# S4 convolution plus gated MLP on one core: a new written-out order of 1281 tasks, with the Exp table, the identity and one token block's statistics moved

## The chip, the cores and the metric

The kernel runs on one core of a Trainium2 chip. The metric is device time in microseconds (us) of one execution. Three runs of the kernel before took 268.34 us in the median (267.07 to 268.83).

## What is computed

A token matrix u (2048 tokens x 512 channels, bfloat16) is layer-normalised to xn. Two branches read xn, and the result is u + A(xn) + B(xn).

```
xn = (x - mean) / sqrt(var + 1e-5)
# A: a diagonal state-space model as a long convolution, per channel d
dt = exp(log_dt);  K[d, l] = Re sum_n C[d,n] * exp(dt[d] * (A_re + i A_im)[d,n] * l) * dt[d] * B[d,n]
yA = irfft(rfft(xn, 4096) * rfft(K, 4096))[:2048] + xn * Dskip
# B: a gated MLP with 1792 hidden units
yB = (sigmoid(xn @ w_gate) * (xn @ w_up)) @ w_down
```

## The kernel before, in words

**Layer norm.** The tokens lie in four groups (`xg`, 0 to 3) of four blocks of 128 tokens. A block's statistics come from VectorE's batch-norm instruction (`stat`, L443, for group 0 with an aggregation, L445) or, for blocks 1 and 3 of group 0, as an alternative from three ACT instructions that sum as they go (`stat_act`, L449 to L451). Group 0's reciprocal deviation is computed on VectorE (`rstd0`, L457 to L470). That of group 1, and that of groups 2 and 3 together, is computed on GpSimd (`rstd`, 33 small instructions each, L479 to L510). Then each block is normalised (`norm` on VectorE, L514, or `norm2` on ACT, L519). Groups 0 and 1 are transposed on PE (L524), groups 2 and 3 by DMA transposes from SP's queue (L547), into `xnT`.

**Parameters.** `params` computes dt with ACT's Exp (L596), scales the identity with it to `dg` (L597, on VectorE), and multiplies the raw parameters by it on PE (L608, banks `ptd` and `pb`); C is only transposed there (L613, `ptp`, evicted as `raw`). Exponentials (L621), a range reduction on VectorE (`turns`, `frac`, L632 to L637), an Abs (L646) and Sin (L640, L641) on ACT give the complex base powers, which are squared (L663 to L672) and multiplied to tables `M` and `B`. ACT loads three function tables: Exp (ahead of the warm-up in L594), Sin, Sigmoid (at L807).

**The two branches.** Eight chunks of 64 channels: `tables` builds the powers H and G by doubling on VectorE (L1244 to L1246, with squares on ACT and VectorE, L888 to L892), PE multiplies them to the kernel K (`pk`, L976), the spectrum steps follow (L762 `pz` for x, L946 to L1026 for K, L1078 `px`), products in the frequency domain (L1125 `pkf`, L1145, L1133 and L1136 `pv`), and the way back (L1192, L1206 to L1212, `ptv`, `py`). The gated MLP runs over four groups of 512 tokens and seven pairs of hidden tiles: `pg` and `pu` on PE (L781), a sigmoid of `pg` on ACT (L807), an eviction of `pu` on ACT, the product on VectorE (L814 or L819), then the down product `po` (L785), its evictions `gs` and `gl`, and an accumulating DMA from GpSimd's queue (L840). `pg` and `pu` share two buffers, so a pair cannot start before the evictions of the pair before it.

**The order.** Nothing is scheduled when the kernel is built. Each `add` makes a task, numbered in the order of the calls, with an engine, a planned cost in us and perhaps an alternative (another engine, cost and function). `TURN` is the written-out order in which the tasks are emitted, and so the order of the instructions on every engine's in-order queue and of the DMA issues on SP's, ACT's and GpSimd's. `OTHER` lists the tasks that take their alternative. A planner that is not part of the kernel made both from the planned costs; when the kernel is built, the costs themselves do nothing:

```python
def order(self):
    for t in (self.tasks[n] for n in OTHER):
        t.eng, t.cost, t.fn = t.alt[:3]
    return [self.tasks[n] for n in TURN]
```

Waits come from the data and the buffers. Tasks that are spoken of later: 0 and 1 load x's blocks 0-1 (SP) and 2-3 (ACT), 2 the identity, 3 the constant s1 (both GpSimd), 4 log_dt, 5 to 10 the raw parameters (6, 10 and 8 on ACT), 11, 12, 14, 15 and 18 to 21 the gate and up weights, 13, 16 and 17 x's groups 1, 2 and 3 (SP). 26 to 29 are group 0's statistics, 30 is rstd0, 43 and 60 are GpSimd's two rstd. 101 fills constants on GpSimd, 103 is the Exp warm-up, 104 dt, 105 dg, 106 to 110 PE's parameter products.

Of the kernel before, what the change touches and what calls it, by code (L numbers as in the profile page):

```python
# [13 lines left out]
ACT = mybir.ActivationFunctionType  # L14
# [237 lines left out]
class _Kernel:  # L252
# [180 lines left out]
    def layernorm(self):  # L433
        nc, add, c = self.nc, self.p.add, self.mult
# [92 lines left out]
        for lo, hi in ((0, 1), (1, 2), (2, 4)):  # L527
            st = [add("DVE", 0.69 if lo else 0.87, lambda i=i: stat(i), [self.ld[f"x{i // 4}{i // 2 * 2 if i < 4 else 0}"]],
                      R["LN2"] + i if lo else R["LN"], use=[self.xg[i // 4]], alt=("ACT", 1.5, lambda i=i: stat_act(i), R["LN"]) if i in (1, 3) else None)
                  for i in range(4 * lo, 4 * hi)]  # L530
            slow = lambda lo=lo, hi=hi: rstd(lo, hi, nc.gpsimd)
            r = add("POOL", 20.0, slow, st, R["LN2"] + 10 * lo) if lo == 1 else add(
                "DVE", 4.2 if lo else 3.4, (lambda lo=lo, hi=hi: rstd(lo, hi, nc.vector)) if lo else rstd0, st, R["LN2"] + 10 * lo if lo else R["LN"],
                alt=("POOL", 16.0, slow, R["LN2"] + 10 * lo) if lo else None)
# [697 lines left out]
def _level(nc, l, o, m, tB, rs, step):  # L1232
# [124 lines left out]
```

## Time and profile before

| what | value |
|---|---|
| time, median of 3 (range) | 268.34 us (267.07 to 268.83) |
| the profiled execution's own time | 268.08 us |
| its span in the trace | 266.3 us |
| PE busy, 2040 matmuls | 236.8 us (89%) |
| VectorE (DVE) busy, 450 instructions | 240.3 us (90%) |
| ACT busy, 369 instructions | 227.8 us (86%) |
| GpSimd (POOL) busy, 107 instructions | 65.7 us (25%) |
| moved by DMA | 44.38 MB, mean 167 GB/s |
| granted TensorE clock, mean | 0.99 |

How to read it: the span is the profiled time between the first and the last instruction; the execution's own time is 1.78 us longer. A row of a timeline has its start, its length, the engine, the line of the kernel, the operation with output and input tiles, and in square brackets the idle time of the engine before it with what ended that. PE, PEld (PE's weight loads), DVE, ACT, POOL and SP are the engines; a q behind a name is its sequencer, which issues DMAs. The chain that ended last is the way back from the last instruction: at each step to what released it, or else to the instruction before it on its engine. Since all engines are in-order, an instruction that waits holds up everything behind it on its engine.

### The profile page before, as it was taken

The page shows a single profiled execution, that of the slowest core. Times are in us where ns is not written, and L with a number is a line of the kernel's source. Part 1 is how long each engine was busy: PE and PEld are TensorE (multiplying, and loading weights), DVE is VectorE, ACT ScalarE, POOL GpSimd, SP SyncE. Part 2 cuts the span into 40 slices and gives each one's busy share as a digit, 9 for nine tenths or more (in the row PEclk, how much of TensorE's full clock was granted, in tenths as well). Part 3 has the DMA queues.
Part 4 walks back from the last instruction along what each step waited for, and adds up shares of the span by engine and source line. Part 5 has one row for each costly group of instructions (what it writes and reads, how often), then busy time and mean ns, then how long its engine had stood idle before and what let it go on. Part 6 is the DMA issues. An engine that isn't in the chain of part 4 may idle for free.

```text
span 266.3 us, 5528 instructions
## 1 busy us (share of the span) xinstructions
PE 236.8 (89%) x2040; PEld 137.4 (52%) x2040; DVE 240.3 (90%) x450; ACT 227.8 (86%) x369; POOL 65.7 (25%) x107
## 2 busy tenths in 40 slices
PE   0556899998799999999999999999998988988992
PEld 0432345443345545545544654665656575567771
DVE  1699999996999999999999999999999999986860
ACT  3989999979987864799897599999999989998851
POOL 4007977884300003100000210000001020207451
PEclk9999999999999999999999999999999999979998
DMA  7729977101692114589424579888798997979898
GB/s 223 265 81 295 337 232 223 39 2 15 166 258 76 54 40 56 101 183 190 131 87 152 115 166 209 233 216 224 193 272 185 290 218 200 245 152 174 172 95 99
DMA packets 75467, 44.38 MB, mean 167 GB/s; under 512 B 40064, under 2 KB 72064, under 8 KB 74928
## 3 DMA queue, kind: packets, MB, share of 16 engines
q1 hardware_dynamic: 66000, 39.66, 54.7%
q0 software_dynamic: 6752, 3.31, 11.8%
q10 hardware_dynamic: 2688, 1.05, 1.6%
q8 instruction: 16, 0.26, 0.4%
q14 instruction: 11, 0.09, 0.1%
HBM read 24.61 MB, written 15.73 MB: 151 GB/s over the span
## 4 chain that ended last, share of the span: by engine, by line
PE 44%; DVE 21%; ACT 20%; POOL 6%; issue 5%; DMA 1%; ACTq 0%; DVEq 0%; POOLq 0%
PE pg L781 11%; PE pu L781 10%; PE po L785 5%; DVE tB L1244 4%; PE pk L976 4%; DVE G L1245 3%; ACT M L361 2%; PE pv L1136 2%; DVE G L1246 2%; DVE H L1245 2%; ACT hT L807 2%; PE pz L762 2%; PE py L1209 2%; PE pv L1133 2%; PE pkf L1125 2%
## 5 line engine op out<-in xcount | busy, mean ns | idle before, releaser
L781 PEld LDWEIGHTS <-W 128*128 128x128 bf16 x448 | 43.2, 98 | 55.5 <-issue 8.2
L781 PE MATMUL pg<-xnT,W 128*128 128x512 bf16 x224 | 52.9, 379 | 4.0 <-ACT hT L807 3.3
L781 PE MATMUL pu<-xnT,W 128*128 128x512 bf16 x224 | 52.9, 379 | 1.7 <-DVE db L658 1.4
L840 POOL DMA_DIRECT2D out_dram<-gs x16 | 13.7, 874 | 156.9 <-ACT gs L361 94.7
L785 PE MATMUL po<-wd,hT 128*128 128x512 bf16 x224 | 51.2, 379 | 0.0
L785 PEld LDWEIGHTS <-hT 128*128 128x128 bf16 x224 | 21.4, 98 | 22.8 <-issue 0.2
L888 ACT ACTIVATE tB<-G 128x1024 bf16<-128x1024 bf16 (+2 forms) x25 | 30.4, 1214 | 3.1 <-DVE G L892 2.5
L807 ACT ACTIVATE hT<-pg 128x1024 bf16<-128x1024 f32 x28 | 29.3, 1045 | 1.8 <-DVE hT L814 0.8
L361 ACT ACTIVATE hT<-pu 128x1024 bf16<-128x1024 f32 x24 | 24.9, 1039 | 1.3 <-PE pu L781 1.2
L1246 DVE TENSOR_TENSOR G<-G,tB 128x512 bf16<-128x512 bf16 (+2 forms) x35 | 22.3, 641 | 0.3
L1245 DVE TENSOR_TENSOR G<-G,M 128x512 bf16<-128x512 bf16 (+2 forms) x50 | 20.5, 451 | 0.1
L976 PEld LDWEIGHTS <-G 128*128 128x128 bf16 x512 | 17.4, 98 | 4.4 <-DVE G L1246 1.0
L976 PE MATMUL pk<-H,G 128*128 128x64 bf16 x512 | 18.4, 193 | 1.1 <-ACT B L361 0.7
L361 ACT ACTIVATE zs<-pz 128x512 bf16<-128x512 f32 x30 | 17.3, 609 | 2.3 <-PE pz L762 2.3
L1145 DVE TENSOR_TENSOR M<-XX,M 128x1024 bf16<-128x1024 bf16 x28 | 18.9, 684 | 0.3 <-ACT M L361 0.3
L1244 DVE TENSOR_TENSOR tB<-G,M 128x512 bf16<-128x512 bf16 (+2 forms) x27 | 18.9, 705 | 0.2
L1246 DVE TENSOR_TENSOR H<-H,tB 128x512 bf16<-128x512 bf16 (+2 forms) x24 | 18.6, 775 | 0.2
L361 ACT ACTIVATE M<-pkf 128x512 bf16<-128x512 f32 x26 | 16.7, 659 | 0.9 <-PE pkf L1125 0.9
L361 ACT ACTIVATE ksb<-pk 128x512 bf16<-128x512 f32 x28 | 16.5, 627 | 0.9 <-PE pk L978 0.7
L814 DVE TENSOR_TENSOR hT<-hT 128x1024 bf16<-128x1024 bf16 x24 | 16.4, 684 | 0.6 <-ACT hT L361 0.5
L361 ACT ACTIVATE Z<-pzk 128x512 bf16<-128x512 f32 x23 | 13.7, 616 | 2.6 <-PE pzk L946 2.6
L1133 PE MATMUL pv<-M,w 128*128 128x256 bf16 (+1 forms) x128 | 14.6, 251 | 1.1 <-DVE M L1145 1.1
(206 smaller groups left out, 477.3 us busy)
## 6 DMA issues: line engine op xcount, KB each, us to landing
z_scr<-zs SPq DMA_DIRECT2D x32, 128.0 KB, 1.8
XX<-XX SPq DMA_DIRECT2D x28, 128.0 KB, 4.1
zk_scr<-Z SPq DMA_DIRECT2D x3, 1024.0 KB, 7.0
B<-zk_scr SPq DMA_DIRECT2D x12, 256.0 KB, 4.4
B<-z_scr SPq DMA_DIRECT2D x8, 256.0 KB, 3.4
wd<-in_B_w_down_dram SPq DMA_DIRECT2D x1, 1792.0 KB, 13.0
xg<-in_A_u_dram SPq DMA_DIRECT2D x3, 512.0 KB, 5.7
W<-in_B_w_up_dram SPq DMA_DIRECT2D x3, 512.0 KB, 7.0
```

What stands on the lines that cost most here:

```text
L361: return self.p.add("ACT", cost, lambda: nc.scalar.activation(out=dst(), in_=src(), func=ACT.Identity), alt=alt and ("DVE", alt[0], lambda ...
L781: nc.tensor.matmul(p[:, kk, :], w(kt, kk), xnT[:, kt, :], start=(kt == 0), stop=(kt == KT - 1))
L785: nc.tensor.matmul(po[:], hT[:, k, jj * 128:(jj + 1) * 128], wd[:, k, :], start=(k == 0), stop=False)
L807: e1 = add("ACT", 1.03, lambda hT=hT, k=k, pg=pg: nc.scalar.activation(out=hT[:, k:k + 2, :], in_=pg[:], func=ACT.Sigmoid), [m1] + held.ge ...
L814: prods.append(add("DVE", 0.69, lambda hT=hT, u=u, k=k: nc.vector.tensor_tensor(out=hT[:, k:k + 2, :], in0=hT[:, u:u + 2, :], in1=hT[:, k: ...
L888: a = add("ACT", 0.22 + 4 * h * k / 1200.0, lambda: nc.scalar.activation(out=sv(), in_=G[:, :, rs, src, :], func=ACT.Square, scale=float(2 ...
L976: nc.tensor.matmul(pk[:, r], G[:, comp, 8 * q + r].rearrange("p a h -> p (a h)"), H[:, comp, 8 * q + r].rearrange("p b h -> p (b h)"), sta ...
L1133: nc.tensor.matmul(pv[:, n, :], w, pp[:, i, n, :], start=(i == 0), stop=(i == 1))
L1145: d = add("DVE", 0.69, lambda pp=pp, XX=XX, k1=k1, bs=bs: nc.vector.tensor_tensor(out=pp[:], in0=XX[:, :, bs, dx], in1=k1[:].to_broadcast( ...
L1244: lambda: [tt(out=tv()[:, c], in0=l[:, c], in1=mul[1][:, c], op=ALU.mult) for c in cs],
L1245: lambda: [tt(out=inner(o[:, c]), in0=inner(l[:, c]), in1=both(c), op=ALU.mult) for c in ones],
L1246: lambda: [tt(out=o[:, c], in0=o[:, c], in1=tv()[:, flip(c)], op=ALU.add) for c in cs],
```

## The change

Three planned costs are set anew: ACT's statistics of a block from 1.5 to 1.75 us, GpSimd's rstd of group 1 from 20.0 to 19.2 and of groups 2 and 3 from 16.0 to 20.0, rstd0 from 3.4 to 3.35. These numbers do not reach the instructions. `TURN` and `OTHER` are replaced, and with them the order on all engines. In the opening:

- ACT: the Exp warm-up (103) and dt (104) stand ahead of ACT's fifth load issue (8) instead of behind it.
- GpSimd: the identity (2) and s1 (3) are issued first, the constants (101) are filled after them.
- Block 1's statistics (27) go from ACT to VectorE, and stand first there; block 3's (29) stay on ACT.
- PE: the last `pb` product (109) stands ahead of the first `pz` (184) instead of behind it.
- SP: x's group 2 (16) is loaded after three writes of `z_scr` and the weight loads 11, 12 and 15, instead of ahead of them.

Further on, all 1281 tasks are in a new order, and 77 tasks besides 27 change sides between their two forms, mostly evictions between ACT and VectorE. In the middle of the kernel, four of the copies `H<-B` and `G<-B` that start a table (L906) go from VectorE to ACT, and two the other way; several evictions of `pk`, `pz` of K and `px` go from ACT to VectorE. ACT's norms of groups 2 and 3 (L519, tasks 61, 71, 81, 92, 72, 91) stand behind the evictions of three of group 0's four `po` tiles; before, 71, 62, 82 and 92 stand behind the first of these alone, and 62 and 82 are VectorE's now, 81 ACT's. The same values are computed from the same inputs; VectorE has three aggregations (L445) in place of two, and ACT one set of statistics instructions (L449 to L451) in place of two.

```diff
-  ... alt=("ACT", 1.5, lambda i=i: stat_act(i), R["LN"]) if i in (1, 3) else None)
+  ... alt=("ACT", 1.75, lambda i=i: stat_act(i), R["LN"]) if i in (1, 3) else None)
...
-            r = add("POOL", 20.0, slow, st, R["LN2"] + 10 * lo) if lo == 1 else add(
-                "DVE", 4.2 if lo else 3.4, (lambda lo=lo, hi=hi: rstd(lo, hi, nc.vector)) if lo else rstd0, st, R["LN2"] + 10 * lo if lo else R["LN"],
-                alt=("POOL", 16.0, slow, R["LN2"] + 10 * lo) if lo else None)
+            r = add("POOL", 19.2, slow, st, R["LN2"] + 10 * lo) if lo == 1 else add(
+                "DVE", 4.2 if lo else 3.35, (lambda lo=lo, hi=hi: rstd(lo, hi, nc.vector)) if lo else rstd0, st, R["LN2"] + 10 * lo if lo else R["LN"],
+                alt=("POOL", 20.0, slow, R["LN2"] + 10 * lo) if lo else None)
...
 TURN = (
-    0, 4, 102, 101, 1, 5, 6, 7, 10, 2, 8, 9, 103, 22, 13, 3, 17, 16, 26, 104, 27, 105, 29, 28, 106, 112, 107, 30,
-    114, 111, 115, 113, 110, 121, 11, 108, 117, 116, 36, 31, 184, 23, 32, 109, 185, 118, 187, 33, 188, 175, 120, 172,
...
+    0, 4, 102, 2, 1, 5, 6, 3, 7, 10, 9, 103, 104, 27, 26, 22, 101, 105, 8, 29, 28, 106, 111, 107, 112, 113, 114, 115,
+    110, 13, 17, 30, 121, 11, 108, 109, 117, 116, 36, 31, 184, 32, 187, 185, 118, 175, 33, 176, 172, 119, 34, 177,
+    186, 188, 120, 12, 173, 189, 35, 122, 15, 41, 37, 16, 42, 14, 166, 39, 174, 123, 40, 18, 38, 43, 181, 20, 124,
...
 OTHER = (
-    27, 29, 38, 44, 60, 61, 62, 71, 72, 82, 91, 92, 143, 144, 145, 148, 149, 155, 158, 160, 161, 227, 239, 301, 316,
...
+    29, 38, 49, 60, 61, 71, 72, 81, 91, 92, 144, 146, 148, 155, 158, 160, 161, 224, 257, 306, 361, 371, 416, 497,
...
```

More of the change, by code (lines that the diff above doesn't have):

```diff
@@ L528, in layernorm @@
             st = [add("DVE", 0.69 if lo else 0.87, lambda i=i: stat(i), [self.ld[f"x{i // 4}{i // 2 * 2 if i < 4 else 0}"]],
-                      R["LN2"] + i if lo else R["LN"], use=[self.xg[i // 4]], alt=("ACT", 1.5, lambda i=i: stat_act(i), R["LN"]) if i in (1, 3) else None)
+                      R["LN2"] + i if lo else R["LN"], use=[self.xg[i // 4]], alt=("ACT", 1.75, lambda i=i: stat_act(i), R["LN"]) if i in (1, 3) else None)
                   for i in range(4 * lo, 4 * hi)]
             slow = lambda lo=lo, hi=hi: rstd(lo, hi, nc.gpsimd)
-            r = add("POOL", 20.0, slow, st, R["LN2"] + 10 * lo) if lo == 1 else add(
-                "DVE", 4.2 if lo else 3.4, (lambda lo=lo, hi=hi: rstd(lo, hi, nc.vector)) if lo else rstd0, st, R["LN2"] + 10 * lo if lo else R["LN"],
-                alt=("POOL", 16.0, slow, R["LN2"] + 10 * lo) if lo else None)
+            r = add("POOL", 19.2, slow, st, R["LN2"] + 10 * lo) if lo == 1 else add(
+                "DVE", 4.2 if lo else 3.35, (lambda lo=lo, hi=hi: rstd(lo, hi, nc.vector)) if lo else rstd0, st, R["LN2"] + 10 * lo if lo else R["LN"],
+                alt=("POOL", 20.0, slow, R["LN2"] + 10 * lo) if lo else None)
             self.rstd.append(r)
```

119 rows, old and new, of tables (OTHER, TURN) are left out of this document.

## The prediction

> **What bounds the kernel now.** I read the page, then the table of stages, then the chain of work, then the rows at the places the chain names. The page first: its span, and the busy tenths in 40 slices of 6.7 us.
>
> ```profile
> span 266.3 us, 5528 instructions
> PE   0556899998799999999999999999998988988992
> DVE  1699999996999999999999999999999999986860
> ACT  3989999979987864799897599999999989998851
> ```
>
> No engine is idle for long: PE, VectorE and ACT stand at 8 to 9 tenths nearly throughout. What is left lies at the start, around slice 9 (60 to 67 us), and in the tail. The stages show it in us (length, then busy time of PE, PE's weight loads, VectorE, ACT, GpSimd, each with its count of instructions):
>
> ```profile
> 0.00:20.00 20.00, 7.54 (x43) 5.91 (x44) 12.30 (x39) 13.96 (x27) 3.25 (x11) 1.00 0.60 190
> 20.00:41.00 21.00, 17.51 (x83) 7.69 (x81) 20.59 (x25) 20.80 (x26) 16.07 (x33) 1.00 0.95 290
> 62.00:90.00 28.00, 25.26 (x179) 12.63 (x178) 24.95 (x45) 24.59 (x36) 3.16 (x4) 1.00 0.52 129
> 90.00:130.00 40.00, 39.95 (x285) 20.26 (x283) 39.17 (x72) 31.73 (x51) 3.38 (x4) 1.00 0.54 115
> 160.00:200.00 40.00, 39.67 (x326) 24.21 (x324) 39.88 (x67) 39.19 (x64) 0.00 (x0) 1.00 0.90 224
> ```
>
> PE loses 12.5 us in the first 20, 3.5 in the next 21, none from 41 to 62, 2.7 from 62 to 90, and then it is full, and VectorE with it. So a microsecond won before 90 us reaches the end only if both PE and VectorE win it. The chain (start, length, what) goes through the opening on ACT and VectorE, then through GpSimd:
>
> ```profile
> 0.72 3.36 DMA ldt<-in_A_log_dt_dram
> 4.52 1.28 ACT L594
> ...
> 8.82 0.82 ACT junk L451 x2
> ...
> 18.03 0.98 ACT zs L361 x2
> 19.01 1.80 ACT cs L646
> ...
> 40.02 1.21 DVE stats L443 x2
> 41.30 0.91 POOL agg L479
> ```
>
> The rows at those places, from the timelines:
>
> ```profile
> 4.10 0.39 ACTq L354 DMA_DIRECT2D rawn<-in_A_C_im_dram  x1
> 6.43 0.69 DVE L597 TENSOR_TENSOR dg<-ident,dtb 128x512 bf16<-128x512 bf16 x1 [1.58 <-DMA ident<-c_ident]
> 9.67 0.17 DVE L458 CAST v_b<-mv 128x4 bf16<-128x4 f32 x1 [0.91 <-ACT junk L451]
> 60.34 1.52 ACT L519 ACTIVATE xg<-xg,nb,rinv 128x512 bf16<-128x512 bf16 x2 [2.04 <-POOL nb L510]
> 65.43 0.29 DVE L362 CAST gl<-po 128x128 bf16<-128x128 f32 x1 [1.94 <-ACT gs L361]
> 69.15 1.89 PE L781 MATMUL pg<-xnT,W 128*128 128x512 bf16 x8 [1.85 <-ACT hT L807]
> ```
>
> ACT's fifth load issue waits until 4.10, just after the first load landed at 4.08, and the Exp table stands behind it. The diagonal dg waits for the identity. At 60.3 GpSimd's second rstd (41.30 to 60.31, 19.0 us; the plan gave it 16) holds ACT for 2.04, and through late evictions VectorE for 1.94 and PE for 0.90 and 1.85.
>
> **The change, part by part: the opening.** ACT ends its fourth issue at 2.67. Now the table follows: 1.28, the warm-up 0.20, dt 0.1 (ldt has landed at 4.08), so dtb is ready at 4.4 instead of 6.11; the fifth issue goes at 4.4 instead of 4.10. Its load then lands 0.3 later, by its 4.8 about 9.2, and holds PE's ptp transposes (8.75 before) for some 0.5; that ends before anything waits for raw. The Trainium skill (ScalarE: Activation LUTs, What ACT_TABLE_LOAD costs) adds a drain of about 1.38 us to each load of 1.28; here the next ACTIVATE starts 0.01 after the load and nothing of 1.38 lies before it, so the trace disagrees, and by the page the fifth issue would be 1.4 later and the opening's gain some 0.5 smaller.
>
> GpSimd issues the identity at about 0.72 instead of 1.71; with the same 4.6 to landing it is there at 5.3 (bounds: 5.3 to 6.3). VectorE has token block 1's statistics as well (0.87, in an idle stretch of 3.08): the x load landed at 3.92, so two blocks end at 5.7, dg runs 5.7 to 6.4 (0.7 earlier), block 2 ends at 7.3. ACT does block 3 alone: x2-3 landed at 5.06, plus its 1.81 gives 6.9. So rstd0 runs from 7.3 without the 0.64 and 0.91 of waiting, 3.35 from its rows, to 10.7 instead of 12.83: 2.1 earlier. Its followers keep that: norms to 12.7, the fractions (1.07 each) to 15.9, against 18.03. On ACT the four exponentials and the scaled copy end at 10.2, the Sin table at 11.5, raw at 12.7; then zs, zs, xnT, zs, zs until 16.0. Before, ACT was at 18.99 there, as pz stood ahead of the last pb on PE and waited 3.50 for a norm; now pb goes first. Abs starts at 16.0 instead of 19.01, the eight sin/cos end at 22.5 (25.53), the first sigmoid ends at 24.9 (27.87): 3.0 earlier.
>
> **SP.** The load of x's group 2 goes from the eighth place to after three zs writes and three W loads. The writes wait for evictions at 13.2 to 15.5, so it is issued near 16.5. Loads of 512 KB took 4.5 to 8.0 to land: 21.0 to 24.5. VectorE wants it at 23.35, so the price is 0 to 1.2; by xg's median 5.7 it is 0. Behind it stand W loads that themselves go out about 3 earlier. The fourth issue and later ones of POOL (memset, dsk) are wanted much later.
>
> **From 25 to 62.** PE runs full from the first sigmoid's end on, so group 0's last po ends at 59.4 instead of 62.4. VectorE has the same work to its last stats (35.8 us of traced durations in both orders), ends it at 38.4 instead of 41.2, and GpSimd's second rstd runs 38.4 to 57.5 by its 19.0. ACT now has 37.8 planned us before the first of the norms that need it instead of 33.9; the old 33.9 took 30.4, so it comes there at 58.8: nothing waits for GpSimd any more. Group 1's first matmuls start at 59.4 (63.69). ACT then does five norms (0.7 each), a copy and two evictions, and reaches the sigmoid at 63.4, so the second pg starts at 64.4 (69.15): PE is 4.7 earlier. One pz that waited 0.90 there is moved away.
>
> **VectorE after that.** I add the traced durations of all instructions that stand ahead in each order. At the same step of the tables (before: 87.4) both orders have 49.3 us since the last stats, so VectorE gains 2.8 there if its 3.05 of idling stays, 5.8 if all goes; the causes (ACT late at 60 to 67) go, so I take 5. Later the new order has 1.4 to 1.6 more VectorE work ahead (copies to tables moved to ACT, but more evictions of pk, ksb and px on VectorE); ACT has about 1 less. VectorE is 98 to 99.7% busy from 90 to 230, so this comes off: 3.4 to 3.6 of the 5 is left. PE's 4.7 is above that, so VectorE decides.
>
> **The tail.** The same instructions in another order. PE idles 10.3 us from 200 on (2.85, 2.22, 5.20 in the three last stages). Nothing shows the new order's waits; I take 0.3 lost for it and for x2 together, bounds 1.5 either way. Sum: 5.0 - 1.5 - 0.3 = 3.2 won. The profiled execution took 268.08 (span 266.3, 1.78 around it), which is 0.26 under the median 268.34. So 268.08 - 3.2 = 264.9.
>
> **Rivals.** 1. GpSimd's second rstd takes longer in its new place. Its rows are no fixed size: the same operation takes 0.20 or 2.15, the long ones at 26 to 32 just while VectorE runs its 2.3 us f32 operations. Should it take 22 (19.0 and 1.4 more such blocked rows of 2.15), it ends at 60.4, ACT waits 1.6 as before and the second gain goes, with what VectorE gained from it: only the opening's 2.9 less 1.5 is left, 266.7. For it: the chain now overlaps other VectorE work. Against: the two rstd took 18.3 and 19.0 among quite different neighbours, and it has 1.3 in hand. The Trainium skill (SBUF — State Buffer, the section on the two sides and the shared port) says that VectorE and GpSimd take a shared port pair exclusively for a whole instruction; the stretched rows agree with it.
> 2. VectorE gains only the opening (2.8), as other waits take the place of the 3.05 of idling: less 1.5 that is 1.3, 266.8. For it: product and table steps are shuffled by several us against each other. Against: none of the old causes is left.
> 3. Slower, by one place: a last step of chunk 6's H table (L1246) has 10.0 us more work ahead on VectorE, and PE's pk of that chunk (L976, 235.0 before) stands in order ahead of all that follows, with 2.5 less PE work ahead. If VectorE has gained nothing by then, the step ends at 235.7 while PE is there at 227.8; the rest (31.3, and the 2.5 put behind it) gives a span of 269.5, a time of 271.3. It decides once some 3.2 of VectorE's remaining 3.5 are lost. For it: VectorE is full for 140 us, so nothing is made up. Against: the opening's 2.1 on VectorE is seen row by row.
> 4. The change does not do what it says: the identity lands at 6.3 as before. Then dg starts at 6.4 as before, block 2 ends at 8.0, and rstd0 ends at 11.4, still 1.4 earlier: 0.7 of the gain goes, 265.6.
>
> **Chances.** Forecast 264.9: 0.46 (own range 262.5 to 265.6). Rival 1: 0.17. Rival 2 with rival 4: 0.23. Rival 3: 0.14. A measurement of this kernel can tell about 1% (2.7 us) from no change: faster is under 265.66, slower over 271.0. So faster 0.46, same 0.40, slower 0.14. The range is 262.5 (the tail's 1.5 and 0.9 of the VectorE idling that I kept) to 269.5, which leaves rival 3 and a little out.
>
> **What would show it.** Right: dtb ready near 4.4, dg near 5.7, rstd0's end near 10.7, Abs near 16.0, first sigmoid near 24, second rstd ending near 57.5 with no ACT wait on it, group 1's second pg near 64.4, and VectorE idle under 1 us from 62 to 70. Wrong: stats waiting for x2 at 23, ACT waiting for GpSimd near 58, PE waiting at L976 for G or H steps from 130 on, or a longer stretch of half PE clock than the one in 230 to 250 (0.91 there).

## The result, and the profile after

The changed kernel takes 265.0 us in the median of four runs (264.1 to 265.24), the kernel before 267.7 in the four runs beside it. The ratio is 0.9888, with a 95% interval of 0.9842 to 0.9935: faster by some 3 us. A ratio compares the executions in the fast state alone, so it need not be the quotient of the medians beside it. The profiled execution took 264.99, its span is 263.1.

The profile page of the changed kernel, span and busy tenths:

```profile
span 263.1 us, 5533 instructions
PE   0849999997999999899999999999999988798991
DVE  3898999999999999799999999999999999998761
ACT  4999999999997953799896699999999989999850
```

VectorE's 6 at the tenth digit (60 to 67 us) is gone; a 7 stands at the seventeenth instead (105 to 112 us). The stages of the changed kernel (length, then busy time of PE, PE's weight loads, VectorE, ACT, GpSimd):

```profile
0.00:20.00 20.00, 9.10 (x49) 6.49 (x50) 15.21 (x45) 15.29 (x26) 4.16 (x18) 0.94 0.65 191
20.00:41.00 21.00, 20.41 (x92) 8.92 (x90) 20.18 (x25) 20.47 (x26) 15.16 (x29) 0.90 0.85 268
62.00:90.00 28.00, 26.55 (x186) 13.30 (x184) 27.54 (x49) 25.26 (x35) 2.79 (x4) 1.00 0.65 171
90.00:130.00 40.00, 38.92 (x306) 20.24 (x305) 37.86 (x66) 29.95 (x46) 3.53 (x4) 1.00 0.41 87
160.00:200.00 40.00, 39.87 (x344) 25.30 (x343) 39.90 (x66) 39.15 (x67) 0.86 (x1) 1.00 0.84 217
```

From 62 to 90 VectorE now idles 0.46 us instead of 3.05. From 90 to 130 something is given back: PE idles 1.08 instead of 0.05, VectorE 2.14 instead of 0.83. The timelines of the changed kernel at the places that the prediction named, and at those where it gives back:

```profile
2.69 1.28 ACT L594 ACT_TABLE_LOAD   x1 [2.69 <-issue]
3.99 0.20 ACT L594 ACTIVATE tiny<-tiny 128x1 f32<-128x1 f32 x1
...
5.64 0.68 DVE L597 TENSOR_TENSOR dg<-ident,dtb 128x512 bf16<-128x512 bf16 x1
...
23.66 0.69 DVE L443 BATCH_NORM_STATS2 stats<-xg 128x6 f32<-128x512 bf16 x1 [0.72 <-DMA xg<-in_A_u_dram]
...
38.60 0.91 POOL L479 TENSOR_TENSOR agg<-stats 128x16 f32<-128x16 f32 x1 [3.80 <-DVE stats L443]
39.47 4.00 POOL L480 TENSOR_TENSOR agg<-stats 128x8 f32<-128x8 f32 x1
...
59.77 0.81 ACT L519 ACTIVATE xg<-xg,nb,rinv 128x512 bf16<-128x512 bf16 x1 [0.57 <-POOL nb L510]
...
65.42 1.89 PE L781 MATMUL pg<-xnT,W 128*128 128x512 bf16 x8 [1.45 <-ACT hT L807]
...
106.97 0.63 ACT L361 ACTIVATE H<-B 128x512 bf16<-128x512 bf16 x1 [2.89 <-PE pk L978]
...
110.06 0.38 PE L762 MATMUL pz<-xg,s 128*128 128x512 bf16 x1 [0.81 <-ACT zs L361]
...
111.53 0.29 DVE L890 TENSOR_TENSOR G<-tB 128x256 bf16<-128x256 bf16 x1 [1.60 <-ACT tB L888]
```

The kernel before had in the second of these rstd rows:

```profile
42.16 2.17 POOL L480 TENSOR_TENSOR agg<-stats 128x8 f32<-128x8 f32 x1
```

The reader is to see four things. The table load starts at 2.69, where ACT's fourth issue ends, and dg no longer waits for the identity. GpSimd's second rstd starts 2.70 earlier than before (41.30), but its second instruction takes 4.00 instead of 2.17 (the next one starts 3.28 after it, before 2.14), and ACT, which comes for the result at 59.20, still waits 0.57. The second pg of group 1 starts 3.73 earlier (69.15 before). And at 107 a copy that went from VectorE to ACT stands in front of a sigmoid and waits 2.89 for PE, so that PE waits for zs, and VectorE for tB, behind it.

### The profile page after: what moved, and what is told of

Its sections match the earlier page's. It is cut to its first block, busy times and chain, and to the rows that moved or that the text cites. A ratio compares the mean times of both kernels' runs of the same rounds, so it can differ in the third digit from the quotient of the medians.

```text
span 263.1 us, 5533 instructions
## 1 busy us (share of the span) xinstructions
PE 238.5 (91%) x2040; PEld 137.8 (52%) x2040; DVE 242.7 (92%) x454; ACT 225.6 (86%) x362; POOL 65.9 (25%) x107
## 4 chain that ended last, share of the span: by engine, by line
PE 40%; DVE 24%; ACT 12%; DMA 9%; POOL 7%; issue 3%; SPq 2%; DVEq 0%; POOLq 0%
PE pg L781 8%; PE po L785 7%; PE pu L781 7%; DVE tB L1244 4%; DMA xt<-in_A_u_dram 3%; PE pk L976 3%; DMA B<-zk_scr 3%; PE pv L1133 3%; DVE G L1245 2%; PE pkf L1125 2%; SPq L354 2%; DMA vp<-v_scr 2%; PE pv L1136 2%; DVE hT L814 2%; DVE stats L443 2%
## 5 line engine op out<-in xcount | busy, mean ns | idle before, releaser
L781 PEld LDWEIGHTS <-W 128*128 128x128 bf16 x448 | 43.8, 99 | 54.3 <-issue 8.3
L781 PE MATMUL pg<-xnT,W 128*128 128x512 bf16 x224 | 54.6, 388 | 4.0 <-ACT hT L807 2.0
L781 PE MATMUL pu<-xnT,W 128*128 128x512 bf16 x224 | 53.6, 383 | 0.2 <-ACT hT L361 0.2
L785 PEld LDWEIGHTS <-hT 128*128 128x128 bf16 x224 | 21.3, 98 | 23.5 <-issue 0.7
L888 ACT ACTIVATE tB<-G 128x1024 bf16<-128x1024 bf16 (+2 forms) x25 | 29.7, 1189 | 1.4 <-DVE G L1246 0.9
L361 ACT ACTIVATE M<-pkf 128x512 bf16<-128x512 f32 x28 | 17.7, 645 | 2.3 <-PE pkf L1125 2.2
L976 PEld LDWEIGHTS <-G 128*128 128x128 bf16 x512 | 17.6, 98 | 3.3 <-issue 0.7
L1244 DVE TENSOR_TENSOR tB<-G,M 128x512 bf16<-128x512 bf16 (+2 forms) x27 | 18.9, 705 | 0.1
L976 PE MATMUL pk<-H,G 128*128 128x64 bf16 x512 | 18.5, 193 | 0.1
L1227 POOL DMA_DIRECT2D out_dram<-M x8 | 11.1, 1480 | 25.7 <-DVE M L1145 12.3
L814 DVE TENSOR_TENSOR hT<-hT 128x1024 bf16<-128x1024 bf16 x24 | 16.3, 684 | 0.1
L1245 DVE TENSOR_TENSOR H<-H,M 128x1024 bf16<-128x1024 bf16 (+1 forms) x16 | 15.2, 953 | 0.1
```

The costliest lines, as they stand in the source:

```text
L361: return self.p.add("ACT", cost, lambda: nc.scalar.activation(out=dst(), in_=src(), func=ACT.Identity), alt=alt and ("DVE", alt[0], lambda ...
L781: nc.tensor.matmul(p[:, kk, :], w(kt, kk), xnT[:, kt, :], start=(kt == 0), stop=(kt == KT - 1))
L785: nc.tensor.matmul(po[:], hT[:, k, jj * 128:(jj + 1) * 128], wd[:, k, :], start=(k == 0), stop=False)
L814: prods.append(add("DVE", 0.69, lambda hT=hT, u=u, k=k: nc.vector.tensor_tensor(out=hT[:, k:k + 2, :], in0=hT[:, u:u + 2, :], in1=hT[:, k: ...
L888: a = add("ACT", 0.22 + 4 * h * k / 1200.0, lambda: nc.scalar.activation(out=sv(), in_=G[:, :, rs, src, :], func=ACT.Square, scale=float(2 ...
L976: nc.tensor.matmul(pk[:, r], G[:, comp, 8 * q + r].rearrange("p a h -> p (a h)"), H[:, comp, 8 * q + r].rearrange("p b h -> p (b h)"), sta ...
```

## The experiments

Two questions were open: which part brings the 3 us, and where the rest of the head start goes. The opening is early row by row, so the first theory was that it carries the gain alone.

### The opening alone

The kernel before with all four opening moves, and nothing else:

```diff
 TURN = (
-    0, 4, 102, 101, 1, 5, 6, 7, 10, 2, 8, 9, 103, 22, 13, 3, 17, 16, 26, 104, 27, 105, 29, 28, 106, 112, 107, 30,
-    114, 111, 115, 113, 110, 121, 11, 108, 117, 116, 36, 31, 184, 23, 32, 109, 185, 118, 187, 33, 188, 175, 120, 172,
+    0, 4, 102, 2, 3, 101, 1, 5, 6, 7, 10, 9, 103, 22, 13, 17, 16, 27, 26, 104, 8, 105, 29, 28, 106, 112, 107, 30, 114,
+    111, 115, 113, 110, 121, 11, 108, 117, 116, 36, 31, 109, 184, 23, 32, 185, 118, 187, 33, 188, 175, 120, 172, 34,
...
 OTHER = (
-    27, 29, 38, ...
+    29, 38, ...
```

> The kernel before with the opening alone changed: Exp table and dt ahead of ACT's fifth load issue, identity and s1 issued first, block 1's statistics on VectorE, the last pb product ahead of the first pz. All else in the old order. Theory A (the opening is on the path, and all that follows shifts with it): rstd0 ends near 10.5, the first sigmoid starts near 24, GpSimd's second rstd starts 2 to 3 us earlier, ACT's wait for it at 58 (2.04 before) stays, since both move together; the time falls by 2.2 to 2.9 us, 0.8 to 1.1%. Rival B (the opening is hidden by the full engines after it, and the gain comes from the new order after 58 us): the time falls by less than 1 us.

Measured: 0.9973 (0.9945 to 1.0001), 0.7 us, and its interval just reaches no change at all. The first theory falls. Two parts of the opening were tried one at a time: 27 on VectorE, ahead of 26 (with the same line of `OTHER`), and the fifth issue, 8, behind 104.

```diff
-    ... 17, 16, 26, 104, 27, 105, 29, 28, ...
+    ... 17, 16, 27, 26, 104, 105, 29, 28, ...
```

> The kernel before with one move: block 1's statistics from ACT to VectorE. Theory A: ACT's statistics end at 7.9 instead of 9.6, rstd0 at 11.3 instead of 12.8, dg stays at 6.4; the time falls by about 1.3 us. Rival: the dtb and the identity decide the opening, and rstd0 is followed by waits for other things; 0.3 us or nothing.

Measured: 0.9966 (0.9939 to 0.9993).

```diff
-    0, 4, 102, 101, 1, 5, 6, 7, 10, 2, 8, 9, 103, 22, 13, 3, 17, 16, 26, 104, 27, 105, ...
+    0, 4, 102, 101, 1, 5, 6, 7, 10, 2, 9, 103, 22, 13, 3, 17, 16, 26, 104, 8, 27, 105, ...
```

> The kernel before with one move: ACT's fifth load issue behind the Exp table and dt. Theory A: dtb is ready at 4.4, dg still waits for the identity until 6.4, but ACT's two blocks of statistics end at 8.3 instead of 9.6, rstd0 at 11.5; the time falls by about 1.2 us. Rival: with dg held by the identity the table's place is worth nothing, and the fifth load, 0.1 to 0.3 later, costs that much.

Measured: 0.9973 (0.9946 to 1.0). Both parts and all four together give the same 0.7 to 0.9 us, each give or take 0.7: something behind the opening caps it. The trace shows what. In the kernel with the opening alone dtb, dg, rstd0 and the first sigmoid (24.03) are as early as in the changed kernel, to 0.4 us. VectorE and ACT stay 2.0 to 2.8 us early from 26 to 58, and then (timelines of that kernel, GpSimd, ACT and VectorE):

```profile
39.81 3.10 POOL L480 TENSOR_TENSOR agg<-stats 128x8 f32<-128x8 f32 x1
42.88 2.19 POOL L481 TENSOR_SCALAR m_b<-agg 128x8 bf16<-128x8 f32 x1
...
60.07 1.52 ACT L519 ACTIVATE xg<-xg,nb,rinv 128x512 bf16<-128x512 bf16 x2 [4.49 <-POOL nb L510]
...
65.17 0.29 DVE L362 CAST gl<-po 128x128 bf16<-128x128 f32 x1 [3.64 <-ACT gs L361]
```

GpSimd's second rstd starts 2.36 earlier and ends 0.26 earlier (60.04): it takes 21.1 us instead of 19.0. (In the two kernels with one part it started 1.8 earlier and ended 0.3 later, at 60.64 and 60.65.) ACT's norm waits 4.49 for it instead of 2.04, and VectorE idles 3.64 for the evictions behind the norms instead of 1.94. The head start is lost at this one place. The second theory was therefore that this place decides what the opening is worth.

### The place around the second rstd

First, the kernel before with ACT's norms (and VectorE's 81 and 63) put behind the evictions of po (72 and 61 behind the first pair's), and pz 259 behind the first pu, the opening untouched. Then the same with the opening.

```diff
-    ... 307, 71, 308, 165, 315, 62, 306, 82, 24, 299, 92, 312, 142, 300, 81, 72, 485, 495, 317, 494, 497, 318, 487,
-    496, 311, 259, 319, 484, 501, 316, 486, 61, 502, 503, 301, 499, 63, 320, 498, 500, ... 324, 509, 322, 75, 488, ...
+    ... 307, 308, 165, 315, 306, 24, 299, 312, 142, 300, 485, 495, 317, 494, 497, 318, 487, 496, 311, 71, 62, 82, 81,
+    92, 319, 484, 501, 316, 486, 502, 503, 301, 499, 320, 259, 498, 500, ... 324, 509, 322, 61, 63, 72, 75, 488, ...
```

> The kernel before with one place changed, the one around GpSimd's second rstd: ACT's norms 71, 62, 82, 92 (and 72, 61, and VectorE's 81) stand behind the evictions 306, 312, 317 and 311 of group 0's po, 61 and 72 behind the first pair's evictions, and pz 259 behind the first pu. The opening is as before. In the run with the four opening moves alone, all engines were 2.4 to 2.7 us early until 58, then ACT waited 4.49 for GpSimd's second rstd (38.94 to 60.04, 21.1 instead of 19.0) and VectorE idled 3.64: all of the head start went there. Theory S (this place swallows whatever is won before it): the ACT wait of 2.04 and VectorE's idle 1.94 go even without the opening, group 1's second pg comes near 67.4 instead of 69.15; 1.3 to 1.9 us faster, ratio about 0.994. Rival T (the gain of the change comes from its reordering after 68 us or elsewhere, not from here): within 0.5, ratio 0.998 to 1.0.

> The kernel before with the four opening moves and the reordering around the second rstd together; the remaining order is that of before. Theory S: GpSimd still ends near 60, but ACT does evictions until then and waits under 1.5 us, VectorE does not idle there, group 1's first pg starts near 60 and its second near 65; 2.7 to 4 us faster than before, ratio 0.985 to 0.990, that is as fast as the changed kernel: the two parts are worth more together than the sum of each alone (0.7 and 1.3 to 1.9). Rival T: the sum of the parts, at most 1.2 us, ratio 0.995 or above, and the rest of the changed kernel's gain lies in its later order.

Measured: the norms alone 0.9995 (0.9978 to 1.0012), with the opening 0.9940 (0.9914 to 0.9966), 1.6 us. Both miss what the second theory gave. The trace says why: ACT's wait went (0 and 0.74 us), but the square of G that VectorE needs (tB, L888) now stood behind four norms, so VectorE idled there instead. Its row in the kernel with both:

```profile
63.26 0.29 DVE L890 TENSOR_TENSOR G<-tB 128x256 bf16<-128x256 bf16 x1 [2.38 <-ACT tB L888]
```

So a wait of ACT that goes is worth nothing if VectorE waits as long for something else. The place was then tested without moving anything in the order, by shortening the second rstd (with the opening).

```diff
-            for _ in range(3):
+            for _ in range(3 if lo < 2 else 0):
...
-            for _ in range(2):
+            for _ in range(2 if lo < 2 else 0):
```

> The kernel with the four opening moves alone, and GpSimd's second rstd cut from 33 instructions to 15: for the token groups 2 and 3 it leaves out the three Newton passes and the two corrections of the reciprocal. Nothing else is moved. It should then end near 50 instead of 60. Theory S (the end of the second rstd holds the opening's gain): ACT's wait of 4.49 at 60 and VectorE's 3.64 go, and 2.5 to 3.5 us come through to the end: ratio 0.987 to 0.991, where the same kernel with the full rstd had 0.9973. Rival T: PE, full in the long middle, is late for other reasons; within 0.5 of the kernel with the opening alone, ratio 0.996 or above.

Measured: 0.9808 (0.9783 to 0.9833), 5.1 us; GpSimd ended at 50.9, ACT waited for nothing, and VectorE idled 0.46 at this place. With the same order the same opening is worth 0.7 us or lets 5.1 through, by the end of one GpSimd chain. The theory stands, and the price is even above what it gave, since before's own wait goes as well: the 5.1 hold both. How they divide was not measured, as the rstd of 15 was not run without the opening.

The undoing from the other side: the changed kernel with its opening put back.

```diff
-    0, 4, 102, 2, 1, 5, 6, 3, 7, 10, 9, 103, 104, 27, 26, 22, 101, 105, 8, 29, 28, 106, 111, 107, 112, 113, 114, 115,
-    110, 13, 17, 30, 121, 11, 108, 109, 117, 116, 36, 31, 184, 32, ...
+    0, 4, 102, 101, 1, 5, 6, 7, 10, 2, 8, 9, 103, 26, 104, 27, 22, 105, 29, 28, 106, 111, 107, 112, 113, 114, 115,
+    110, 13, 3, 17, 16, 30, 121, 11, 108, 117, 116, 36, 31, 184, 109, 32, ...
```

(27 is back in `OTHER`, and 16 is gone from its later place.)

> The changed kernel with its opening put back: the Exp table behind ACT's fifth issue, identity behind the constants, token block 1's statistics on ACT, pb 109 behind pz 184, x's group 2 loaded early. Its order after that, the norms behind the evictions among it, is the new one. Theory S: the norms no longer wait for GpSimd (whose rstd starts near 41 and may take 19 to 21, to 60.3 to 62.4, with ACT coming there about 61.5), but everything before is 2.7 late again: about 2 to 2.7 us slower than the changed kernel, ratio against before 0.996 to 0.999. Rival T (the opening is worth only the 0.7 us that it gives alone): 0.991 to 0.993.

Measured: 1.0021 (1.0006 to 1.0035), 0.6 us slower than before. In the new order the opening is worth 0.9888 against 1.0021, some 3.6 us; in the old order 0.7. And the new order without it is worth nothing: less than the second theory gave (0.996 to 0.999), so it must lose elsewhere what it wins at this place.

### A ledger of VectorE, and three tests of it

VectorE is taken here as the engine through which these waits reach the end, so two numbers of each trace are set beside its result: how early VectorE is at one step that all kernels have just ahead of the place (the first product of L729, at 60.15 before), and how long it idles from 58 to 74 (2.62 before). Their sum is what VectorE has won by 74. The next two tests were predicted from it. A milder cut of the second rstd, by one of three Newton passes and one of two corrections, with the opening and without:

```diff
-            for _ in range(3):
+            for _ in range(3 if lo < 2 else 2):
...
-            for _ in range(2):
+            for _ in range(2 if lo < 2 else 1):
```

> The kernel before with the four opening moves, and GpSimd's second rstd shortened by one Newton pass and one correction of the reciprocal (7 of 33 instructions; left out is that last refinement of groups 2 and 3's deviation). From the rows of the opening alone (last pass 2.2, last correction 1.6) GpSimd ends near 56.2 instead of 60.0; ACT comes there at 55.6, VectorE at 58.6. Theory L (VectorE's time is the ledger: a gain is what VectorE no longer idles, less the work it is given): the 3.64 and 0.63 that VectorE idled at 59 to 65 are gone, so nearly as fast as with the rstd cut to 15 instructions: ratio 0.981 to 0.985, 262.5 to 263.3 where before has 267.4. Rival Q (the end of the rstd is not sharp, each microsecond of it counts): 60.0 to 56.2 is 38% of the cut to 50.7, so 38% of that kernel's further gain, ratio 0.991.

> The kernel before, its opening untouched, with the second rstd shortened by the same 7 instructions (left out: the last Newton pass and the last correction for groups 2 and 3). GpSimd ends near 56.5 instead of 60.3, ACT comes there at 58.3. Theory L: VectorE's idle 1.94 at 65.4 goes and some of its 0.57, which ACT's wait of 2.04 caused: 1.9 to 2.4 us faster, ratio 0.991 to 0.993; then the opening, worth 0.7 alone, is worth 2.4 to 2.9 on top of this (see the kernel with both). Rival M (before's waits at 60 to 66 are not on the path, as the kernel with only the norms moved, 0.9995, seems to say): ratio 0.998 to 1.0.

Measured: without the opening 0.9916 (0.9890 to 0.9942), as theory L gave. With it 0.9876 (0.9841 to 0.9911), between the two forecasts: ACT still waited 1.51 for GpSimd (57.00) and VectorE 1.38 behind it, more than the 0.6 I had worked out, since ACT came at 55.5 and GpSimd ended at 56.97. With these idle times in the ledger the sum is right (table). The opening was thus worth 1.1 on top of the shorter rstd (0.9916 to 0.9876) and not the 2.4 to 2.9 of the forecast. So the end of the rstd had to be met by the order as well:

```diff
-    ... 307, 71, 308, 165, 315, 62, 306, 82, 24, 299, 92, 312, 142, 300, 81, 72, 485, 495, 317, 494, 497, 318, 487,
-    496, 311, 259, 319, 484, 501, 316, 486, ...
+    ... 307, 308, 165, 315, 306, 24, 299, 312, 142, 300, 485, 495, 317, 71, 62, 82, 81, 92, 494, 497, 318, 487, 496,
+    311, 259, 319, 484, 501, 72, 316, 486, ...
```

> The kernel with the four opening moves and the second rstd shortened by 7 instructions (left out: the last Newton pass and the last correction for groups 2 and 3), in which ACT's norms 71, 62, 82 and 92 stand behind the evictions 306, 312, 317 and the copy 142, and norm 72 behind the square 501 (tB), so that VectorE's table step is not held by them. There GpSimd ended at 56.8 and ACT, waiting since 55.3, idled 1.5, VectorE 1.38 and 0.58. Theory L (VectorE's idle time at 59 to 65 is the price of that place): ACT fills its 1.5 with evictions, the norms run from about 56.9, tB is squared by 61.1, VectorE idles under 0.7 there: ratio 0.980 to 0.984, about 262.5 where before has 267.5, ahead of the changed kernel's 0.9888. Rival K (PE and the later stages take the rest, as when evictions were moved back to ACT in the changed kernel): within 0.4 us of the kernel without the moved norms, 0.986 to 0.989.

Measured: 0.9827 (0.9789 to 0.9865), 262.65 us where before had 267.86. Theory L holds. ACT (its timeline in that kernel) runs the norms without a wait, and the square of G stands ahead of the norms 72 and 61:

```profile
56.95 2.92 ACT L519 ACTIVATE xg<-xg,nb,rinv 128x512 bf16<-128x512 bf16 x4
...
60.45 0.62 ACT L888 ACTIVATE tB<-G 128x512 bf16<-128x512 bf16 x1
60.97 1.51 ACT L519 ACTIVATE xg<-xg,nb,rinv 128x512 bf16<-128x512 bf16 x2
```

This version, before's order with the opening, a shorter rstd and six norms moved, is the fastest of those that keep all work but a refinement; its ratio is below the changed kernel's 0.9888, though the two intervals just overlap (0.9789 to 0.9865 and 0.9842 to 0.9935).

The ledger, in us (measured: 1 minus the ratio, times the median of the kernel before beside it):

| kernel | early at L729 | idle 58 to 74 | won by 74 | measured gain |
|---|---|---|---|---|
| opening alone | 2.69 | 4.95 | 0.4 | 0.7 |
| block 1's statistics on VectorE alone | 2.10 | 4.92 | -0.2 | 0.9 |
| Exp table ahead alone | 2.08 | 4.91 | -0.2 | 0.7 |
| norms alone | -0.04 | 2.47 | 0.1 | 0.1 |
| opening and norms | 3.16 | 3.30 | 2.5 | 1.6 |
| opening, rstd of 15 | 2.42 | 0.60 | 4.4 | 5.1 |
| opening, rstd of 26 | 2.78 | 2.05 | 3.4 | 3.3 |
| rstd of 26 | 0.06 | 0.55 | 2.1 | 2.2 |
| opening, rstd of 26, norms | 2.95 | 0.52 | 5.1 | 4.6 |
| the change | 2.60 | 0.16 | 5.1 | 3.0 |
| the change, opening undone | 0.05 | 0.14 | 2.5 | -0.6 |
| the change, sigmoid ahead | 2.97 | 0.14 | 5.5 | 3.1 |
| the change, four evictions on ACT | 2.91 | 0.16 | 5.4 | 1.8 |

The nine kernels with before's later order bring to the end what they have won by 74, within 1.1; a measured gain is itself sure to 0.4 to 1.3 us only. The four with the new later order lose 2.1 to 3.6 of it. The traces are of single executions, and by these executions' own times (268.08 before) it is the same: the nine keep it within 0.8, the four lose 2.0 to 3.0. How the third column is read, 16 less VectorE's busy time (the third busy number of a line): the window of the kernel before, with 13.38, and that of the kernel with the opening alone, with 11.05,

```profile
58.00:74.00 16.00, 13.26 (x63) 5.99 (x62) 13.38 (x34) 13.93 (x23) 6.67 (x11) 1.00 0.37 86
...
58.00:74.00 16.00, 12.15 (x50) 5.11 (x50) 11.05 (x30) 13.65 (x22) 6.33 (x12) 0.89 0.40 91
```

and the same window of the changed kernel, with 15.84:

```profile
58.00:74.00 16.00, 14.55 (x69) 6.54 (x68) 15.84 (x37) 14.90 (x22) 6.14 (x11) 1.00 0.54 110
```

### What the new later order gives back

Two kernels asked where. The first takes the sigmoid (376) of the place at 107 out from behind the copy (632):

```diff
-    590, 570, 568, 372, 374, 373, 371, 571, 572, 205, 574, 573, 630, 632, 569, 229, 375, 592, 594, 376, 230, 591, ...
+    590, 570, 568, 372, 374, 373, 371, 571, 572, 205, 574, 573, 630, 376, 632, 569, 229, 375, 592, 594, 230, 591, ...
```

> The changed kernel with one move: the sigmoid of group 2's first pg (L807) ahead of the copy H<-B (L906) on ACT, which waits 2.89 us for PE's pk at 104 to 107 us. Theory C (this copy, moved from VectorE to ACT by the change, gives back what was won: it holds the sigmoid, the zs evictions and the square behind it, and so PE for 0.81 and VectorE for 1.60): those two waits shrink by 0.8 to 0.9 each and the time falls by 0.5 to 0.9 us below the changed kernel's. Rival D (the two engines meet the next wait anyway, each full): the same time within 0.3 us.

Measured: 0.9885 (0.9858 to 0.9912), as the changed kernel. VectorE's 1.60 at 111.53 became 0.69, and from 90 to 160 it idled 1.62 instead of 2.52; but from 160 to 230 it idled 1.17 instead of 0.28. What was won there did not arrive, as rival D had it.

The second takes the other term of the prediction, VectorE's added work: four of the evictions that the change gave to VectorE go back to ACT.

```diff
 OTHER = (
-    ... 565, 571, 573, 616, 618, 642, 664, 668, 739, ...
+    ... 565, 571, 573, 642, 739, ...
```

> The changed kernel with four evictions (616, 618, 664, 668, of pk and of K's spectrum, at 124 to 152 us) back on ACT, in the same places of the order: VectorE has 2.7 us less to do between 124 and 152, ACT 2.4 more (it is busy 30 of 40 us in 90 to 130 and 25 of 30 in 130 to 160). Theory L: VectorE is 99% busy from there to 230, so 1.5 to 2.7 us come through, ratio against before 0.979 to 0.983. Rival P (PE, 39.9 of 40 us busy in 160 to 200, decides as well there): within 0.7 of the changed kernel, 0.986 to 0.990. Rival W: slower, if ACT, in order, brings an eviction late and PE waits for the buffer: above 0.991.

Measured: 0.9933 (0.9910 to 0.9956): by the two ratios 1.2 us slower than the changed kernel, though the intervals overlap, and surely not the 0.979 to 0.983 of theory L, which fails here. VectorE's windows in that kernel:

```profile
90.00:130.00 40.00, 38.77 (x305) 20.05 (x303) 36.70 (x63) 30.49 (x48) 3.53 (x4) 1.00 0.41 87
130.00:160.00 30.00, 29.48 (x211) 15.57 (x210) 28.32 (x56) 25.05 (x42) 3.44 (x4) 1.00 0.60 142
```

VectorE idles 3.30 and 1.68 there instead of 2.14 and 0.38: the work that was taken off came back as waiting. Its two new waits end on PE's products `pk`:

```profile
128.49 0.42 DVE L1245 TENSOR_TENSOR G<-B,M 128x512 bf16<-128x512 bf16 x1 [1.06 <-PE pk L978]
...
151.00 0.43 DVE L1245 TENSOR_TENSOR G<-B,M 128x512 bf16<-128x512 bf16 x1 [1.33 <-PE pk L978]
```

By VectorE's last table products (the last row of L1244, at 234.87 before) VectorE has done 221.50 us of work in this kernel, as in the kernel before, and 223.53 in the changed kernel; yet it is there at 233.14, and in the changed kernel at 233.01. So up to that step 2.0 us less of VectorE's work is worth nothing. That PE decides there (rival P) fits; but the evictions were given to ACT, and whether PE's order or ACT holds the `pk` is not separated. The profiled execution takes 0.7 longer than the changed kernel's, mostly behind that step: 30.7 us to the end instead of 30.1. The granted clock was at half around it for 7.0 us (228.4 to 235.4), in the changed kernel for 3.5 (229.0 to 232.5). So that this kernel came out slower need not be the price of the four evictions.

The same step shows where the new order loses. Of the 5.1 won by 74 the changed kernel has 1.9 left there, so 3.2 are gone; the other three with the new later order have lost 3.1 to 3.6, the nine with the old one 0.3 to 1.8. (Behind it the tail of the kernel before is the longer one, 31.4 us against 30.1, so in the end less is missing.) Of the changed kernel's 3.2, 1.1 are more idling of VectorE than before (3.1 us from 74 to the step instead of 2.0) and the rest is more work; in the kernel with the four evictions all 3.6 are idling. The half clock is no rival here: VectorE idles under 0.2 us in the last 7 us up to the step in each of the four.

What causes it stays open. PE idles more from 90 to 230, 5.34 us instead of 3.40; but two kernels with the old later order, whose traces also hold all 2040 matmuls (the rstd of 26 with the opening and without), idle 4.30 and 3.99 there and keep what they won. PE's longest waits there in the changed kernel end on something that ACT delivers (0.81 at 110.06, 1.19 at 212.60, 0.57 at 220.64, 1.03 at 228.44); in the kernels with the sigmoid ahead and with the four evictions on ACT the one at 212 is longer (1.65 and 1.49) and ends on a DMA. That ACT, in order, delivers late would fit a part of this; an order with these four deliveries ahead was not tried.

## Why the prediction came out right, step by step

**The opening: right nearly row by row.** dtb was ready at 4.42 (4.4 predicted), dg started at 5.64 (5.7), rstd0 ended at 10.48 (10.7), Abs started at 16.07 (16.0; its row before starts at 18.88, so it came 2.8 earlier and not 3.0), the first sigmoid ran from 24.04 (near 24). The fifth load held PE's ptp transposes for 0.87 (0.5), and nothing waited for raw. Rival 4 falls: the identity was issued at 1.22, not 0.72, and landed 4.3 later, at 5.5; that is behind dtb but ahead of the end of the two blocks' statistics (5.72), so dg did not wait for it. On the table load, the next ACTIVATE again started 0.02 after it (3.99 behind 2.69 and 1.28). The Trainium skill (ScalarE: Activation LUTs, What ACT_TABLE_LOAD costs) adds a drain of some 1.38; no row here has one.

**SP.** x's group 2 held VectorE for 0.72 at 23.66, inside the 0 to 1.2 of the prediction, which had taken 0. The load took 7.07 to land, not 5.7. It was one of the signs of being wrong, and so was ACT's wait for GpSimd below; neither was large enough to undo the forecast.

**The second rstd: the step that was off.** I took its 19.0 from the one row before and kept 1.3 in hand. It ran 38.60 to 59.74, 21.1 us, and took 21.1 to 21.3 in the other kernels with an early opening and the whole rstd too. The condition of rival 1 came in nearly to its figure (22). What saved the forecast was that ACT arrived at 59.20 with evictions in front of its norms: a wait of 0.57 and not 2.04. GpSimd was 2.2 later than the 57.5 of the prediction; the 1.3 in hand and the 0.4 by which ACT came after its 58.8 took up most of it. That this was enough is luck, as the one row gave no bound. Group 1's second pg started at 65.42 instead of 64.4.

**VectorE to 90: right.** I took 5.0 won, 2.8 from the opening and 2.2 of the 3.05 idle. The ledger has 5.1 (2.60 and 2.46).

**VectorE after that: right in size, by luck, since the cause does not hold.** The prediction let 1.4 to 1.6 come off because VectorE has that much more work and decides from 90 to 230. The work is there (242.74 us of VectorE instead of 240.30, of which 0.88 is block 1's statistics), and 2.1 were lost against 1.8 allowed with the tail's 0.3. But with 2.0 us of such work taken off again (240.7 of VectorE in the whole trace) VectorE reached its last table step no earlier (233.14 against 233.01), and the kernel was not faster (0.9933). "VectorE decides" is the step that failed; VectorE waited for PE's `pk` instead. What does take the 2.1 stays open, so it is luck that the 1.8 came near.

**Rival 3** did not come: in the changed kernel PE shows no wait above 0.2 at L976 from 130 on.

**How the parts go together.** The prediction added the opening and the 2.2 of idling as if each were there without the other. They are not independent: the opening is worth 0.7 without the place at 60 and 3.6 with it, since GpSimd hardly ends earlier when it starts earlier. The sum was right for the change as a whole; it would have been 2 us wrong for its first half alone.

## What to carry to other kernels

A head start is worth only what passes the next fixed point: follow it to the first result that does not move with it (here the end of a GpSimd chain), and see which engine's order stands in front of that. Count idle time on the engine that carries it on, not on the one that waits first: norms moved out of ACT's way gave nothing while VectorE waited as long for the next thing. And that an engine is 98% busy does not say that less work on it helps: take some away and see if it idles instead.

## What the runs showed of the hardware

The same GpSimd instruction on a 128x8 tile (L480) took 2.17 us before, 3.10 in the kernel with the opening alone and 4.00 in the changed kernel (to the start of the next one 2.14, 3.07 and 3.28); on 128x4 in the first rstd it took 0.20. In all three it ran while VectorE had two-input instructions one behind the other (L675, L677, in the last two L814 as well). So the chain is not of a fixed length: in these two kernels, started 2.4 and 2.7 earlier among other VectorE instructions, it ended only 0.3 and 0.6 earlier. The Trainium skill (SBUF — State Buffer, Who interferes with whom) says that of a VectorE instruction with two SBUF inputs and a GpSimd instruction that reads SBUF the second to start blocks until the first ends; the stretched rows agree with it, and which of several VectorE instructions held the 4.00 cannot be read from the rows.

The granted PE clock had a stretch at half in the opening of the changed kernel (0.90 from 20 to 41, the first pg's seven recorded matmuls 3.19 us, where eight take 1.89 at 25.25), which the kernel before did not show. The change is not needed for one: the kernel with only the norms moved, whose first 58 us are those of before, had 0.92 in the same stage.

In the tail the half clock shows in the time of a profiled execution. From VectorE's last row of L1244 to the end, the six kernels with the old later order and no such stretch between 220 and 245 took 29.9 to 30.1 us, the four with one of 3.5 us (the kernel before, 237.0 to 240.5, among them) 30.5 to 31.5. How much it moves a median is open: the twelve runs of the changed kernel with its opening undone have mean clocks from 0.969 to 0.993, and their times, 267.51 to 268.38, show no order by it.
